# A Fourier layer and two expert layers on one core: expert blocks of 512 tokens, more steps of weight conversion for each unit, one subtraction on GpSimd

## The chip, the cores and the metric

One core of a Trainium2 chip runs the whole program. The metric is device time in microseconds (us) of one execution; a kernel's time is the median of several. All times here are in us unless marked ns. The engines are PE (matmuls), DVE (VectorE), ACT (ScalarE), POOL (GpSimd) and SP, which here issues every DMA.

## The reference, cut to what matters

```python
# x: (2, 3008, 256); expert weights 256 x 2048 and 2048 x 256, twice
X = rfft(x, axis=1)
Yr = Xr @ w_r - Xi @ w_i + b_r;  Yi = Xr @ w_i + Xi @ w_r + b_i
Y = soft_shrink(Yr, 0.01) + 1j * soft_shrink(Yi, 0.01)
x = irfft(Y).reshape(6016, 256)
h = x @ moe_w_in;   x = (h * cos(h)) @ moe_w_out
h = x @ moe2_w_in;  return (h * clip(h + 3, 0, 6) / 6) @ moe2_w_out
```

## The kernel before, in words

Nearly every matmul is done in three terms of split numbers: an operand is kept as a high part (rounded by ACT) and a low part (the rest, subtracted by DVE), and high*high, low*high and high*low are added up in PSUM.

**The Fourier half** runs once for each of two batches `b`. Sixteen `a_part`s (lines 329 to 344) make `zp` by the first DFT step and split it into `zh`, `zl`. Then come twelve steps `k2_step(b, p)` (lines 465 to 487). PE does 21 matmuls of 512 columns in each: two `w_mm` (tile `pp`, 6 each), one `v_mm` (tile `vp`, 3) and one `b_mm` (tile `bp`, 6). The other engines carry `bp` of step p-2 through the soft shrink: `bias_add` (DVE, line 426), `shrink_a` (ACT), `shrink_b` (DVE, 435), `shrink_hi` (ACT, makes `sh`, 440), `shrink_lo` (DVE, makes `sl`, 445). `v_mm(b, p)` reads `sh` and `sl` one step later, and `v_store` writes its result to DRAM. The twelve steps of a batch end in `drain`, whose pieces are dealt out among the next `a_part`s or, for the second batch, among the first expert units.

**The inverse DFT** is `y_part(g, ec)` (lines 281 to 302): 8 short matmuls into a buffer `yp` of the PSUM tag `h`, then split into token tiles `tok`. Sixteen groups g of 376 tokens, two halves each. `YP` says at which steps of the second batch the first of them stand; the rest stand among the expert units (`events`), shortly before the block that needs them.

**The expert half.** Tokens are cut into twelve blocks (`BLOCK_TOKENS`). A unit is 128 of the 2048 hidden features for one block in one expert layer m: `mm_h` (6 matmuls into `h`, line 578), four passes of ACT and DVE, and, four units later, `mm_out` (6 matmuls into `acc`, line 635). There are 16 units to a block and a layer, so 384 units. Order: blocks 0 and 1 of the first layer in turns of four units (`IL`), then block 2, then blocks (0, j) and (1, j-3) in turns of one unit, then the last three of the second layer.

**The weights** come as 64-bit numbers and are converted on the chip, 16 pieces of 512 KB for a layer. A piece takes five steps of `cv.step`: DVE operations `clamp` (153), `shift` (156), `top` (159), `exponent` (162), `rest` (165), with `magnitude` and `hi` on ACT (150, 169), and `rest`'s addition and `lo` on POOL (166, 172). `lo` of a piece, after which it counts as finished, comes in the fourth step of the next piece. Steps are dealt out by tables: `RATE_A` in the `a_part`s (one for each pair, from the last pair of the first batch on), `RATE_W` in the k2 steps below `PW` (an entry before `shrink_b`, then one of two in turn), `RATE_M` in the expert units. Where a unit needs a piece that isn't finished, `cv.require` issues the missing steps on the spot.

Each engine executes its instructions in the order in which they were put into its own queue. The orders shown below are those queues.

Of the kernel before, what the change touches and what calls it, by code (L numbers as in the profile page):

```python
# [12 lines left out]
I32 = mybir.dt.int32  # L13
U32 = mybir.dt.uint32
AF = mybir.ActivationFunctionType
ALU = mybir.AluOpType
# [11 lines left out]
LAM = 0.01  # L28
TWO_PI = 2.0 * math.pi
YPAIRS = 4  # L30
BLOCK_TOKENS = [502, 502, 500] * 4
A_CHUNKS = [4] * 8
NFC = DFF // 128
LEAD = 3
DELAY = 4
WARM = 9
IL, IM = 4, 1

RATE_M = (1, 1, 1, 1, 0, 0, 1, 0)
RATE_A = (0, 1)  # L40
RATE_W = (1, 1, 2)
LATE, CC, CV0 = [1, 3, 4], 5, 7
XB = 3
EG, PW = 0, 10
YP = (0, 2, 4, 6, 8)
YE = 3


# [64 lines left out]
def fourier_moe_moe_kernel(ctx, tc, x, w_r, w_i, b_r, b_i, ta, tg, fg, win1, wout1, win2, wout2, out):  # L113
    nc = tc.nc
    pe, act, dve, sp = nc.tensor, nc.scalar, nc.vector, nc.sync

    def f32(ap):
        return ap.bitcast(F32)

    persist = ctx.enter_context(tc.tile_pool(name="persist", bufs=1))  # L120
# [13 lines left out]

    def convert(src, dst_hi, dst_lo, name):

        raw = persist.tile([128, 512, 2], I32, tag="raw", bufs=2, name=f"raw{name}")
        a = persist.tile([128, 512], F32, tag="cva", bufs=2, name=f"cva{name}")
        b = persist.tile([128, 512], F32, tag="cvb", bufs=1, name=f"cvb{name}")
        au, bu = a.bitcast(U32), b.bitcast(U32)  # L140
        w_lo, w_hi = raw.bitcast(U32)[:, :, 0], raw.bitcast(U32)[:, :, 1]

        def load():
            if len(src.shape) == 2:
                sp.dma_start(raw.rearrange("p f two -> p (f two)"), src)
            else:
                sp.dma_start(raw.rearrange("p (a f) two -> p a (f two)", a=2), src)

        def magnitude():
            act.activation(a, raw.bitcast(F32)[:, :, 1], AF.Abs)  # L150

        def clamp():
            dve.tensor_scalar(a, a, T_MIN, T_MAX, op0=ALU.max, op1=ALU.min)

        def shift():
            dve.tensor_scalar(au, au, 3, 0x3FFFFFF8, op0=ALU.logical_shift_left, op1=ALU.bitwise_and)

        def top():
            dve.scalar_tensor_tensor(au, w_hi, 0xC0000000, au, op0=ALU.bitwise_and, op1=ALU.bitwise_or)

        def exponent():
            dve.tensor_scalar(bu, au, 0xFF800000, None, op0=ALU.bitwise_and)

        def rest():
            dve.scalar_tensor_tensor(b, w_lo, float(2.0**-52), b, op0=ALU.mult, op1=ALU.mult)
            nc.gpsimd.tensor_tensor(a, a, b, op=ALU.add)

        def hi():
            act.activation(dst_hi, a, AF.Copy)  # L169

        def lo():
            nc.gpsimd.tensor_tensor(dst_lo, a, f32(dst_hi), op=ALU.subtract)  # L172

        return dict(load=load, magnitude=magnitude, clamp=clamp, shift=shift, top=top, exponent=exponent, rest=rest, hi=hi, lo=lo)
# [72 lines left out]
    cv = Converter()  # L247
# [18 lines left out]
    def token_set(pool, i):  # L266
        return [[pool.tile([128, MAXT], F32R, name=f"tok{i}_{e}{z}") for z in range(2)] for e in range(2)]

    free_sets = [token_set(persist, i) for i in range(3)]

    def load_u(g):
        if g >= NG:
# [32 lines left out]
    with ExitStack() as actx:  # L305
        apool = actx.enter_context(tc.tile_pool(name="apool", bufs=1))
        with tc.manual_schedule(engines={mybir.EngineType.PE, mybir.EngineType.SP, mybir.EngineType.Activation}):
# [134 lines left out]

            def shrink_lo(b, p):
                sh, sl = sh_t[b, p]
                dve.tensor_tensor(sl, u_t.pop((b, p)), f32(sh), op=ALU.subtract)

            def v_mm(b, p):
                vp = psum.tile([128, 2, D], F32, tag="acc1", bufs=2, name=f"vp{b}_{p}")
# [82 lines left out]
                        load_x(NA + p - 6)  # L531
                pend = drain(b)
            pend.pop(0)()
            y_part(2, 0)
            pend.pop(0)()
            y_part(2, 1)
            pend.pop(0)()
            pend.pop(0)()


    mpool = ctx.enter_context(tc.tile_pool(name="mpool", bufs=1))
    with tc.manual_schedule(engines={mybir.EngineType.PE, mybir.EngineType.SP, mybir.EngineType.Activation}):
        free_sets += [token_set(mpool, i) for i in range(3, LEAD + 3)]


        groups = [[(0, 0), (0, 1)]] + [[(0, j)] for j in range(2, LEAD)]
        groups += [[(0, j), (1, j - LEAD)] for j in range(LEAD, NBLK)] + [[(1, j)] for j in range(NBLK - LEAD, NBLK)]
        order, units, events = [], [], {}
        for i, group in enumerate(groups):
            step = IL if i == 0 else IM  # L550
            g0, n0 = len(units), len(order)
            order += group
            for q in range(NFC // step):
                units += [(n0 + n, *job, q * step + f) for n, job in enumerate(group) for f in range(step)]
            size = len(units) - g0
            if i + 1 < len(groups) and groups[i + 1][0][0] == 0:
                parts = [(g, e) for g in groups_of(groups[i + 1][0][1]) for e in range(2)]
                for k, (g, e) in enumerate(reversed(parts)):
                    events.setdefault(g0 + size - YE - 2 * k, []).append(lambda g=g, e=e: y_part(g, e))
# [100 lines left out]
        G = len(units)  # L660
        for g in range(G + DELAY):
# [9 lines left out]
                split_g(g - 2)  # L671
            if 0 <= g - 1 < G:
                act2(g - 1)
            if g > EG:
                cv.step(RATE_M[g % 4])
            for f in pend[:2]:
                f()
            pend = pend[2:]
            if g < G:
                act_abs(g)  # L680
                if g > EG:
                    cv.step(RATE_M[4 + g % 4])
            if 0 <= g - DELAY < G:
                n2, m2, _, fc2 = units[g - DELAY]
                cv.require(("out", m2, fc2 // 2))
# [49 lines left out]
```

## Time and profile before

| | before |
|---|---|
| median of 3 runs | 1264.58 us (1263.5 to 1269.22) |
| profiled execution, its own time | 1263.34 us |
| its span in the trace | 1261.6 us |
| PE busy | 1241.5 us, 98% |
| DVE / ACT / POOL busy | 827.2 / 791.6 / 85.4 us |
| mean granted TensorE clock | 0.985 of full speed |

The span is that of the instructions; 1.7 us of the execution's own time lie outside of it. Busy is the time in which at least one instruction of the engine ran. In the views of the trace a row has the start and the length in us, the engine, the line of the kernel, the operation, and output<-inputs with partitions x elements; `xN` counts instructions, and `[t <-E tile]` is idle time before it with what ended that time.

### The profile page before, as it was taken

To read this page: it belongs to the slowest core of one execution; us is meant where nothing else is said; L and a number is where in the kernel's file an instruction comes from. 1 tells how busy PE (TensorE), PEld (TensorE's weight loads), DVE (VectorE), ACT (ScalarE), POOL (GpSimd) and SP (SyncE) were. 2 spreads that over 40 slices of the span, in tenths; PEclk is the share of its full clock that TensorE was granted. 3 is DMA by queue.
4 is the path that set the end of the run, shared out by engine and by line. 5 is a ranking of instruction groups with operands and counts; after the bars stand their busy time and mean duration, and the time that the engine had idled before them with its cause. 6 is when DMAs were issued, how large, how long until landed. Compare 5 with 4: busy or idle time off the path is not lost.

```text
span 1261.6 us, 15535 instructions
## 1 busy us (share of the span) xinstructions
PE 1241.5 (98%) x5633; PEld 1035.5 (82%) x5633; DVE 827.2 (66%) x1349; ACT 791.6 (63%) x1468; POOL 85.4 (7%) x68
## 2 busy tenths in 40 slices
PE   8999999999998999999999999999999999999998
PEld 7888878888876888888888888888888888888887
DVE  5988889998877655656556556556556556554444
ACT  5665679898775655656666566566666666653443
POOL 0212212222223000000000000000000000000000
PEclk7997999999998999999999999999999999999999
DMA  7354441112111000001001001001000000000000
GB/s 204 91 151 131 124 110 52 51 51 85 51 51 34 17 1 19 17 1 35 17 1 34 1 1 34 1 18 34 1 18 17 1 1 17 1 17 1 17 17 17
DMA packets 25117, 48.53 MB, mean 38 GB/s; under 512 B 2768, under 2 KB 15696, under 8 KB 25040
## 3 DMA queue, kind: packets, MB, share of 16 engines
q1 hardware_dynamic: 25040, 47.54, 13.0%
q8 instruction: 44, 0.72, 0.2%
q14 instruction: 33, 0.27, 0.1%
HBM read 35.08 MB, written 12.45 MB: 38 GB/s over the span
## 4 chain that ended last, share of the span: by engine, by line
PE 94%; DVE 2%; ACT 1%; DMA 1%; issue 1%; POOL 0%; SPq 0%; DVEq 0%; POOLq 0%; ACTq 0%
PE h L578 41%; PE acc L635 41%; PE pp L397 5%; PE bp L420 2%; PE zp L333 2%; PE yp L285 2%; PE vp L451 1%; DMA x<-in_x_dram 1%; DVE zl L344 1%; DVE gl L622 0%; POOL w2i L172 0%; ACT r L589 0%; DVE u L435 0%; ACT r L602 0%; SPq L324 0%
## 5 line engine op out<-in xcount | busy, mean ns | idle before, releaser
L613 DVE SCALAR_TENSOR_TENSOR h<-r,h 128x502 f32<-128x502 f32 (+1 forms) x192 | 131.4, 684 | 261.4 <-ACT r L594 261.3
L578 PE MATMUL h<-tok,w2i 128*128 128x502 f32 (+1 forms) x1152 | 293.7, 389 | 6.3 <-ACT w2i L169 4.8
L578 PE MATMUL h<-tok,w1i 128*128 128x502 f32 (+1 forms) x1152 | 294.4, 391 | 3.5 <-DVE gl L622 3.3
L635 PE MATMUL acc<-gh,w1o 128*128 128x502 f32 (+1 forms) x768 | 267.8, 389 | 0.0
L635 PE MATMUL acc<-gh,w2o 128*128 128x502 f32 (+1 forms) x768 | 267.8, 390 | 0.0
L578 PEld LDWEIGHTS h<-tok,w2i 128*128 128x128 f32 x1152 | 217.2, 189 | 52.3 <-ACT w2i L169 5.5
L622 DVE TENSOR_TENSOR gl<-h,gh 128x502 fp32r<-128x502 f32 (+1 forms) x384 | 258.7, 674 | 0.7 <-ACT gh L621 0.7
L578 PEld LDWEIGHTS h<-tok,w1i 128*128 128x128 f32 x1152 | 214.9, 188 | 46.4 <-DVE gl L622 4.6
L594 ACT ACTIVATE r<-h 128x502 f32<-128x502 f32 (+1 forms) x192 | 113.3, 590 | 183.1 <-PE h L578 182.5
L621 ACT ACTIVATE gh<-h 128x502 fp32r<-128x502 f32 (+1 forms) x384 | 225.2, 586 | 1.2 <-PE acc L635 1.0
L589 ACT ACTIVATE r<-h 128x502 int32<-128x502 f32 (+1 forms) x192 | 113.6, 592 | 149.3 <-PE h L578 146.9
L590 DVE SCALAR_TENSOR_TENSOR r<-r,h 128x502 f32<-128x502 int32 (+1 forms) x192 | 129.9, 677 | 117.0 <-ACT r L589 116.3
L635 PEld LDWEIGHTS acc<-gh,w2o 128*128 128x128 f32 x768 | 145.0, 189 | 28.9
L635 PEld LDWEIGHTS acc<-gh,w1o 128*128 128x128 f32 x768 | 144.5, 188 | 29.3
L635 PE MATMUL acc<-gl,w2o 128*128 128x502 f32 (+1 forms) x384 | 149.9, 390 | 0.0
L635 PE MATMUL acc<-gl,w1o 128*128 128x502 f32 (+1 forms) x384 | 149.7, 390 | 0.0
L602 ACT ACTIVATE r<-r 128x502 f32<-128x502 f32 (+1 forms) x192 | 120.1, 625 | 41.1 <-DVE r L590 41.1
L611 DVE TENSOR_TENSOR h<-r,h 128x502 f32<-128x502 f32 (+1 forms) x192 | 129.6, 675 | 0.0
L610 ACT ACTIVATE r<-r 128x502 f32<-128x502 f32 (+1 forms) x192 | 120.3, 627 | 0.0
L635 PEld LDWEIGHTS acc<-gl,w2o 128*128 128x128 f32 x384 | 72.5, 189 | 15.4
L635 PEld LDWEIGHTS acc<-gl,w1o 128*128 128x128 f32 x384 | 72.1, 188 | 15.6
L333 PE MATMUL zp<-ta,x 96*128 96x96 f32 x256 | 41.6, 338 | 5.5 <-DVE zl L344 4.1
(79 smaller groups left out, 912.3 us busy)
## 6 DMA issues: line engine op xcount, KB each, us to landing
x<-in_x_dram SPq DMA_DIRECT2D x16, 384.0 KB, 4.7
u_dram<-v SPq DMA_DIRECT2D x48, 128.0 KB, 2.4
u_sb<-u_dram SPq DMA_DIRECT2D x16, 384.0 KB, 3.8
raw0i<-in_win_dram SPq DMA_DIRECT2D x8, 512.0 KB, 4.3
raw0o<-in_wout_dram SPq DMA_DIRECT2D x8, 512.0 KB, 3.9
raw1i<-in_win_dram SPq DMA_DIRECT2D x8, 512.0 KB, 3.6
raw1o<-in_wout_dram SPq DMA_DIRECT2D x8, 512.0 KB, 3.7
out_dram<-o SPq DMA_DIRECT2D x16, 251.0 KB, 2.1
```

The lines of the kernel that those rows point to most:

```text
L333: pe.matmul(zp[:, i * ROWS : (i + 1) * ROWS], lhsT=x_t[a][:, i, kc * 128 : (kc + 1) * 128], rhs=ta_t[a][:, i * ROWS : (i + 1) * ROWS], sta ...
L578: pe.matmul(hp[:, :t], lhsT=w[:, c0 : c0 + 128], rhs=r[:, :t], start=(i == 0), stop=(i == 5))
L589: act.activation(k[:, :t], hp[:, :t], AF.Copy, bias=0.0, scale=1.0 / TWO_PI)
L590: dve.scalar_tensor_tensor(r[:, :t], k[:, :t], -TWO_PI, hp[:, :t], op0=ALU.mult, op1=ALU.add)
L594: act.activation(r[:, :t], hp[:, :t], AF.Relu, bias=3.0, scale=1.0)
L602: act.activation(mid[g][:, :t], mid[g][:, :t], AF.Abs)
L610: act.activation(r[:, :t], r[:, :t], AF.Sin, bias=math.pi / 2, scale=-1.0)
L611: dve.tensor_tensor(hp[:, :t], r[:, :t], hp[:, :t], op=ALU.mult)
L613: dve.scalar_tensor_tensor(hp[:, :t], r[:, :t], 6.0, hp[:, :t], op0=ALU.min, op1=ALU.mult)
L621: act.activation(gh[:, :t], hp[:, :t], AF.Copy)
L622: dve.tensor_tensor(gl[:, :t], hp[:, :t], f32(gh[:, :t]), op=ALU.subtract)
L635: pe.matmul(acc[n][d][:, :t], lhsT=w[:, fc % 2, d * 128 : (d + 1) * 128], rhs=r[:, :t], start=(fc == 0 and i == 0), stop=(fc == NFC - 1 an ...
```

## The change

- `BLOCK_TOKENS` becomes eleven blocks of 512 tokens and one of 384 (6016 in all, as before). A token tile has 512 columns instead of 502.
- The first group is no longer two blocks in turns: blocks 0, 1, 2 of the first layer run one after the other.
- Only the first two groups of `y_part` (four parts) stand before the expert units, at steps 3 and 6 and after the drain's first two pieces; before, it was three groups (six parts).
- `RATE_W` is (1, 2, 2) for all twelve steps (`PW` 12): three conversion steps for each k2 step instead of 2 or 3 in ten of twelve. In the expert units the rate is 7 steps for 8 units while blocks 0 to 2 run, then one for a unit of the first layer and two for one of the second.
- The raw weights have three buffers instead of two.
- `shrink_lo` runs on POOL instead of DVE.

```diff
-BLOCK_TOKENS = [502, 502, 500] * 4
+BLOCK_TOKENS = [512] * 11 + [384]
...
-IL, IM = 4, 1
-RATE_M = (1, 1, 1, 1, 0, 0, 1, 0)
 RATE_A = (0, 1)
-RATE_W = (1, 1, 2)
+RATE_W = (1, 2, 2)
+RATE_1 = ((1, 0),) * 7 + ((0, 0),)
+RATE_2 = ((1, 0), (1, 1))
...
-EG, PW = 0, 10
-YP = (0, 2, 4, 6, 8)
+PW = 12
+YP = (0, 3, 6)
...
-        raw = persist.tile([128, 512, 2], I32, tag="raw", bufs=2, name=f"raw{name}")
+        raw = persist.tile([128, 512, 2], I32, tag="raw", bufs=3, name=f"raw{name}")
...
-    free_sets = [token_set(persist, i) for i in range(3)]
+    free_sets = [token_set(persist, i) for i in range(2)]
...
-                dve.tensor_tensor(sl, u_t.pop((b, p)), f32(sh), op=ALU.subtract)
+                nc.gpsimd.tensor_tensor(sl, u_t.pop((b, p)), f32(sh), op=ALU.subtract)
...
-            y_part(2, 0)
+            y_part(1, 0)
             pend.pop(0)()
-            y_part(2, 1)
+            y_part(1, 1)
...
-        groups = [[(0, 0), (0, 1)]] + [[(0, j)] for j in range(2, LEAD)]
+        groups = [[(0, j)] for j in range(LEAD)]
...
-            step = IL if i == 0 else IM
...
-            for q in range(NFC // step):
-                units += [(n0 + n, *job, q * step + f) for n, job in enumerate(group) for f in range(step)]
+            for q in range(NFC):
+                units += [(n0 + n, *job, q) for n, job in enumerate(group)]
...
-            if g > EG:
-                cv.step(RATE_M[g % 4])
+            rate = (0, 0)
+            if g < G:
+                rate = RATE_1[g % 8] if units[g][2] < LEAD and units[g][1] == 0 else RATE_2[units[g][1]]
+            cv.step(rate[0])
...
-                if g > EG:
-                    cv.step(RATE_M[4 + g % 4])
+                cv.step(rate[1])
```

In the changed file the lines of the Fourier half stand one further down (`bias_add` is line 427, `shrink_lo` 446), those of the expert half one further up.

The first place is DVE's queue in the k2 steps of the first batch. The names: `bp` bias_add, `u` shrink_b, `ph` the low part of a `pp`, `sl` shrink_lo, `cva`/`cvb` conversion. Before:

```order
L426 TENSOR_TENSOR bp_3_487<-bp_3_487,bias 128x512
L162 TENSOR_SCALAR cvb0o_369<-cva0o_368 128x512
L165 SCALAR_TENSOR_TENSOR cvb0o_369<-raw0o_367,cvb0o_369 128x512
L435 SCALAR_TENSOR_TENSOR u_3_504<-bp_3_487,u_3_504 128x512
L411 TENSOR_TENSOR ph_0_5_495<-pp_10_496,ph_0_5_494 128x512
L445 TENSOR_TENSOR sl_3_515<-u_3_504,sh_3_514 128x512
L426 TENSOR_TENSOR bp_4_535<-bp_4_535,bias 128x512
L411 TENSOR_TENSOR ph_0_5_495<-pp_11_522,ph_0_5_494 128x512
L435 SCALAR_TENSOR_TENSOR u_4_552<-bp_4_535,u_4_552 128x512
```

And in the changed kernel, around `bp` 5 and 6:

```order
L427 TENSOR_TENSOR bp_5_594<-bp_5_594,bias 128x512
L412 TENSOR_TENSOR ph_0_6_548<-pp_13_576,ph_0_6_547 128x512
L157 TENSOR_SCALAR cva0i_511<-cva0i_511 128x512
L436 SCALAR_TENSOR_TENSOR u_5_615<-bp_5_594,u_5_615 128x512
L412 TENSOR_TENSOR ph_0_7_606<-pp_14_607,ph_0_7_605 128x512
L160 SCALAR_TENSOR_TENSOR cva0i_511<-raw0i_510,cva0i_511 128x512
L163 TENSOR_SCALAR cvb0i_512<-cva0i_511 128x512
L166 SCALAR_TENSOR_TENSOR cvb0i_512<-raw0i_510,cvb0i_512 128x512
L412 TENSOR_TENSOR ph_0_7_606<-pp_15_633,ph_0_7_605 128x512
L427 TENSOR_TENSOR bp_6_645<-bp_6_645,bias 128x512
L436 SCALAR_TENSOR_TENSOR u_6_666<-bp_6_645,u_6_666 128x512
```

The `sl` rows have left DVE's queue, and more conversion rows stand between the shrink's.

The second place is POOL's queue in the same steps, which holds only conversion before (the additions of `rest`, and `lo`):

```order
L166 TENSOR_TENSOR cva0i_249<-cva0i_249,cvb0i_250 128x512
L166 TENSOR_TENSOR cva0o_368<-cva0o_368,cvb0o_369 128x512
L172 TENSOR_TENSOR w1i_68<-cva0i_249,w1i_67 128x512
L166 TENSOR_TENSOR cva0o_459<-cva0o_459,cvb0o_460 128x512
L172 TENSOR_TENSOR w1o_82<-cva0o_368,w1o_81 128x512
```

And in the changed kernel:

```order
L167 TENSOR_TENSOR cva0o_343<-cva0o_343,cvb0o_344 128x512
L446 TENSOR_TENSOR sl_3_522<-u_3_505,sh_3_521 128x512
L167 TENSOR_TENSOR cva0o_434<-cva0o_434,cvb0o_435 128x512
L173 TENSOR_TENSOR w1o_82<-cva0o_343,w1o_81 128x512
L446 TENSOR_TENSOR sl_4_569<-u_4_557,sh_4_568 128x512
L446 TENSOR_TENSOR sl_5_626<-u_5_615,sh_5_625 128x512
L173 TENSOR_TENSOR w1o_84<-cva0o_434,w1o_83 128x512
```

Each `sl` now stands among the conversion's operations, here `sl_4` behind two of them.

The third place is ACT's queue where the expert units begin; `r` and `gh` are tiles of the first units, `sh_11` and `u_11` of the last shrink. Before:

```order
L431 ACTIVATE u_11_1661<-bp_11_1628 128x512
L589 ACTIVATE r_1721<-h_1714 128x502
L440 ACTIVATE sh_11_1725<-u_11_1661 128x512
L602 ACTIVATE r_1721<-r_1721 128x502
L589 ACTIVATE r_1736<-h_1729 128x502
```

And in the changed kernel:

```order
L432 ACTIVATE u_11_1685<-bp_11_1652 128x512
L588 ACTIVATE r_1757<-h_1750 128x512
L170 ACTIVATE w1o_93<-cva0o_1431 128x512
L441 ACTIVATE sh_11_1763<-u_11_1685 128x512
L601 ACTIVATE r_1757<-r_1757 128x512
L588 ACTIVATE r_1774<-h_1767 128x512
```

One `hi` of the conversion has come to stand among the first unit's operations.

## Rows read from the trace of the kernel before

**Rows 1.** The page: busy time of each engine with its share of the span, and the granted TensorE clock in tenths, in 40 slices of the span.
```profile
PE 1241.5 (98%) x5633; PEld 1035.5 (82%) x5633; DVE 827.2 (66%) x1349; ACT 791.6 (63%) x1468; POOL 85.4 (7%) x68
PEclk7997999999998999999999999999999999999999
```

**Rows 2.** Busy time by stretch of the span: the stretch, its length, then busy time (and instructions) of PE, PEld, DVE, ACT and POOL, the granted clock, the DMA share and GB/s.
```profile
40.00:80.00 40.00, 40.00 (x176) 32.83 (x175) 36.50 (x62) 26.51 (x49) 10.61 (x8) 1.00 0.46 128
...
360.00:400.00 40.00, 33.65 (x139) 26.53 (x138) 30.93 (x51) 23.56 (x44) 13.52 (x10) 0.91 0.14 40
...
440.00:480.00 40.00, 40.00 (x177) 33.04 (x177) 23.16 (x38) 24.41 (x45) 0.00 (x0) 1.00 0.00 1
```

**Rows 3.** The chain of work that ended last, in order of time, in the k2 steps of the first batch: one step.
```profile
43.61 1.39 PE pp L397 x6
45.00 1.36 PE bp L420 x6
46.36 1.36 PE pp L397 x6
47.72 0.70 PE vp L451 x3
```

**Rows 4.** The same chain in the expert half: a unit of 502 tokens, and one of 500.
```profile
453.43 1.38 PE acc L635 x6
454.81 1.35 PE h L578 x6
...
1224.27 1.34 PE acc L635 x6
1225.61 1.35 PE h L578 x6
```

**Rows 5.** The timeline at 377 us, PE's rows.
```profile
377.21 0.38 PE L635 MATMUL acc<-gh,w1o 128*128 128x502 f32 x1
378.98 0.72 PE L578 MATMUL h<-tok,w2i 128*128 128x502 f32 x2 [1.38 <-ACT w2i L169]
380.87 0.50 PE L578 MATMUL h<-tok,w2i 128*128 128x502 f32 x1 [1.16 <-POOL w2i L172]
384.74 1.21 PE L578 MATMUL h<-tok,w2i 128*128 128x502 f32 x2 [3.37 <-ACT w2i L169]
386.29 0.79 PE L578 MATMUL h<-tok,w2i 128*128 128x502 f32 x1 [0.34 <-POOL w2i L172]
...
389.39 1.81 PE L578 MATMUL h<-tok,w1i 128*128 128x502 f32 x6
391.04 0.39 PE L635 MATMUL acc<-gh,w1o 128*128 128x502 f32 x1
```

**Rows 6.** The timeline of the k2 steps of the first batch, rows of DVE and, last, the matmul that reads `sl`.
```profile
57.98 0.42 DVE L153 TENSOR_SCALAR cva0o<-cva0o 128x512 f32<-128x512 f32 x1
58.43 0.69 DVE L411 TENSOR_TENSOR ph<-pp,ph 128x512 fp32r<-128x512 f32 x1
...
62.35 0.69 DVE L165 SCALAR_TENSOR_TENSOR cvb0o<-raw0o,cvb0o 128x512 f32<-128x512 uint32 x1
62.96 0.68 DVE L435 SCALAR_TENSOR_TENSOR u<-bp,u 128x512 f32<-128x512 f32 x1
...
64.34 0.69 DVE L445 TENSOR_TENSOR sl<-u,sh 128x512 fp32r<-128x512 f32 x1
65.62 0.70 DVE L426 TENSOR_TENSOR bp<-bp,bias 128x512 f32<-128x512 f32 x1 [0.59 <-PE bp L420]
...
67.02 0.39 PE L451 MATMUL vp<-sl,fgr 128*128 128x512 f32 x1
```

**Rows 7.** The timeline at three places at which DVE and POOL run at once.
```profile
63.18 1.30 POOL L166 TENSOR_TENSOR cva0o<-cva0o,cvb0o 128x512 f32<-128x512 f32 x1 [6.11 <-DVE cvb0o L165]
63.56 0.68 DVE L411 TENSOR_TENSOR ph<-pp,ph 128x512 fp32r<-128x512 f32 x1
...
192.76 1.29 POOL L172 TENSOR_TENSOR w1o<-cva0o,w1o 128x512 fp32r<-128x512 f32 x1 [8.33 <-ACT w1o L169]
192.92 1.41 DVE L162 TENSOR_SCALAR cvb0i<-cva0i 128x512 uint32<-128x512 uint32 x1
...
384.76 1.47 POOL L172 TENSOR_TENSOR w2i<-cva1i,w2i 128x512 fp32r<-128x512 f32 x1 [0.74 <-ACT w2i L169]
385.14 1.64 DVE L165 SCALAR_TENSOR_TENSOR cvb1o<-raw1o,cvb1o 128x512 f32<-128x512 uint32 x1
```

**Rows 8.** The timeline where the expert units begin: the fifth unit's first matmuls, and an operation of the conversion on ACT.
```profile
182.39 1.62 PE L578 MATMUL h<-tok,w1i 128*128 128x502 f32 x6 [1.58 <-DVE gl L622]
182.40 0.65 ACT L169 ACTIVATE w1o<-cva0o 128x512 fp32r<-128x512 f32 x1
```

**Rows 9.** The timeline of PE around two parts of the inverse DFT, one behind the other, in the first expert units.
```profile
247.88 1.03 PE L285 MATMUL yp<-tg_sb,u_sb 96*128 96x94 f32 x8
249.73 1.62 PE L578 MATMUL h<-tok,w1i 128*128 128x502 f32 x6 [0.82 <-DVE gl L622]
...
255.26 1.03 PE L285 MATMUL yp<-tg_sb,u_sb 96*128 96x94 f32 x8
256.07 1.61 PE L578 MATMUL h<-tok,w1i 128*128 128x502 f32 x6
```

More of the change, by code (lines that the diff above doesn't have):

```diff
@@ L542, in fourier_moe_moe_kernel @@
     with tc.manual_schedule(engines={mybir.EngineType.PE, mybir.EngineType.SP, mybir.EngineType.Activation}):
-        free_sets += [token_set(mpool, i) for i in range(3, LEAD + 3)]
-        groups = [[(0, 0), (0, 1)]] + [[(0, j)] for j in range(2, LEAD)]
+        free_sets += [token_set(mpool, i) for i in range(2, LEAD + 3)]
+        groups = [[(0, j)] for j in range(LEAD)]
         groups += [[(0, j), (1, j - LEAD)] for j in range(LEAD, NBLK)] + [[(1, j)] for j in range(NBLK - LEAD, NBLK)]
```

## The prediction

> **What bounds the kernel now.** The page's first part comes first: PE is busy 98% of the span and no other engine over 66% [rows 1]. So the end moves only if PE runs fewer or shorter matmuls, or if it loses less time to waiting and to the lower clock. The change leaves the number of matmuls as it is. The stretches show where PE is not full: from 440 to 480 us it runs 177 matmuls at full clock, from 360 to 400 only 139, at a granted clock of 0.91 [rows 2]. The k2 steps are full as well, but there DVE is busy 36.50 of 40 us [rows 2]: an engine that is not the bound and has little to spare. The chain of work gives the rhythm: a k2 step takes 1.39 + 1.36 + 1.36 + 0.70 = 4.81 us [rows 3], an expert unit of 502 tokens 2.73, one of 500 2.69 to 2.71 [rows 4].
>
> **The gap at 377 us, and what the faster conversion does to it.** From 377.21 to 391.04 PE gets through 19 matmuls of 502 columns [rows 5]. At 2.73 / 12 = 0.2275 each they need 4.3, so 13.8 - 4.3 = 9.5 us are lost: idle 6.2, the rest matmuls that start 0.4 apart after the idle, where the stretch's clock has fallen. The rows name who ended the waits: `hi` (ACT) and `lo` (POOL) of a weight piece `w2i`. Counting steps tells why. Before the first unit stand 1 + 8 + 2 x 25 = 59 steps, then 1.25 for each unit. Unit 73 is the first that reads the last quarter of `w2i`, pieces 29 and 30 of 32; piece 30 is finished with step 30 x 5 + 4 = 154, and 59 + 1.25 x 72 is 149. Five steps short: `require` issues them on the spot and PE waits through the whole piece. In the changed kernel 1 + 8 + 2 x 36 = 81 steps stand before the first unit, 42 come in units 0 to 47, then 1.5 for each unit: 154 is reached at unit 69, three units (8 us) early. The first layer's weights have their 80 steps before the units begin, so that running block 0 alone, which takes them twice as fast, costs nothing. Gain: **-9.5**.
>
> **Longer blocks.** Matmuls and columns are as many as before, but time does not go by columns: six of 512 columns take 1.36 us (`bp`) or 1.36 to 1.39 (`pp`) [rows 3], where six of 502 take 1.35 (`h`) and 1.38 (`acc`) [rows 4]. Three of `vp` take 0.70, or 1.40 for six [rows 3]. `vp` reads `sh` and `sl`, which lie in the very buffers (tags `gh`, `gl`) that `mm_out` reads. So I take 1.365 for `h` and 1.40 for `acc`, 2.765 for a unit of 512. The block of 384 has no row; with three quarters of 2.765 (2.07) as the lower bound and 128 columns less at 1/2.4 ns each (2.765 - 0.64 = 2.125) as the upper, I take 2.10. Before: 32 units x (8 x 2.73 + 4 x 2.70) = 1044.5. After: 32 x (11 x 2.765 + 2.10) = 1040.5. That is **-4**; if `acc` went like `bp` it would be 32 x 11 x 0.04 = 14 less, and if `h` went like the slower `pp` (1.39) 9 more.
>
> **Subtraction on GpSimd and three steps for each k2 step.** Rows of DVE that take 0.69 start 0.61 apart, rows of 0.42 start 0.45 apart [rows 6]. A piece is 3 x 0.45 + 2 x 0.61 = 2.57, a step 0.51. Before, DVE has 5 x 0.61 + 2.5 x 0.51 = 4.3 for a k2 step; after, 4 x 0.61 + 3 x 0.51 = 3.97, so that 0.84 of 4.81 are free. On DVE's own account the move pays for the conversion. But POOL takes 1.30 for a subtraction or addition [rows 7], so it gets 1.30 + 3/5 x 2 x 1.30 = 2.86 for a step, 59%, where it had 1.30. And the two engines get in each other's way: an `exponent` of DVE that begins 0.16 after a POOL operation takes 1.41, where operations of its kind take 0.42, and ends 0.28 after it; a `rest` takes 1.64 instead of 0.69 [rows 6, 7]. A `ph` beside POOL takes 0.68, as ever [rows 7]: what reads PSUM isn't held up. So each of the three conversion operations of a step finds POOL at work with a chance of 0.59 and then waits half of 1.30: 3 x 0.59 x 0.65 = 1.15. That is 0.31 over the 0.84 that are free. Twenty k2 steps carry both (the first two of a batch have no shrink yet): **+6**. The lower end is 0 (the waits fall into idle time), the upper comes from waits as long as the one shown (about 1.0, so 1.77 for a step): 0.93 x 20 = 19. A second way to the same loss is the path of `sl`: now it ends at 65.03 and `vp` reads it at 67.02 [rows 6], 2.0 spare. On POOL it takes 0.6 longer, and one operation in front of it 1.3 more; with two in front, as `sl_4` has them, 1.2 are missing. Queued behind that `vp` is all of PE.
>
> The Trainium skill (SBUF — State Buffer, section Who interferes with whom) says that DVE instructions in a two-port mode or with two SBUF inputs and GpSimd's share a port pair as an exclusive lock, and that whoever issues first keeps it for the whole instruction. That is what the rows show. Taken only as a budget, the rule asks for 3 x 0.51 + 2.86 = 4.4 of port time in a step of 4.81 and would charge nothing, which is the first rival's time; it does not say how two queues in fixed order share it.
>
> **Smaller things.** Where units begin, the fifth unit waits 1.58 for the first unit's `gl` [rows 8], at the end of a chain through ACT; a `hi` of 0.65 [rows 8] now stands in that chain: **+0.6** (0 to 2, since `y_part(1, 1)` is also needed by the very first unit now). The first `y_part` of a cluster among single units costs 1.85, the second 0.81 [rows 9]. There are three such clusters instead of two: **+1** (0 to 2). The third raw buffer and six more small splits lie beside PE's work: nothing, as long as ACT and DVE keep their gaps in the units.
>
> **Sum.** -9.5 - 4 + 6 + 0.6 + 1 = -5.9. Against the profiled execution's own 1263.3 that is 1257.4; the median of the three runs shown is 1.2 above it, so I say 1258.5.
>
> **The rivals.**
> - *The port costs nothing* (the k2 step stays at 4.81): the terms without +6 give 1251 to 1253. For it: DVE has 0.84 to spare and the port's sum is below a step. Against it: both queues are in fixed order, and the port would be taken 91% of the time.
> - *`acc` takes 1.36 too*: 14 less, 1244. For it: six matmuls of 512 columns do go in 1.36 [rows 3]. Against it: the only rows that read those buffers, `vp`, don't.
> - *Slower: the k2 steps become DVE's and POOL's.* If nearly every conversion operation waits a full POOL operation and `sl` comes late on top, the step goes to about 5.9: 20 x 1.1 = 22, which gives 1275. It decides from 5.75 for a step on, where the loss passes 19. For it: at 384.76 both engines do just this, operation by operation [rows 7]. Against it: 2.44 of DVE's work in a step don't touch the port and can run beside POOL.
> - *The wait for `w2i` stays* (a piece is late for another reason, such as its load): 1268. The count leaves three units, so this is unlikely.
>
> **How the numbers follow.** About 0.5% (6.3 us) is what a measurement of this kernel can tell from no change, so faster means below 1258.3 and slower above 1270.9. The forecast's mechanism, with k2 losing 3 to 16 us (1255 to 1268), gets 0.51, spread from its lower end; the first rival (1250 to 1255) 0.24; the second (1242 to 1250) 0.10; the slower one 0.13; the last 0.02. Faster: 0.24 + 0.10 and 0.14 of the forecast's own, 0.48. Slower 0.13, the same 0.39. The range 1246 to 1271 leaves out the slower rival and half of the second: 0.18. The forecast's own range is 1255 to 1268.
>
> **What would show it.** Right: no PE wait on `w2i`, and no gap at unit 73; six `acc` of 512 in 1.40 and six `h` in 1.36 to 1.37; k2 steps on the chain of 4.9 to 5.5, with conversion rows of DVE over 1.0 us beside POOL's and waits of `vp` on POOL `sl`. Wrong: k2 steps of 4.81 to the end (the +6 falls), six `acc` in 1.36 (the -4 is too small), or PE below full clock in the k2 steps after such waits, which the sum does not hold at all.

## The result: 1.1% slower

The changed kernel takes **1279.64 us** (median of four runs, 1276.8 to 1281.3); the kernel before took 1265.45 beside it. The ratio is **1.0106, 95% interval 1.0074 to 1.0138**, 14 us more where 6 less were forecast. It lies above the range of 1246 to 1271.

The page of the changed kernel, its parts 1, 2 and 4 (busy time, the granted clock in tenths, the chain that ended last):
```profile
PE 1258.8 (98%) x5633; PEld 1039.5 (81%) x5633; DVE 823.9 (64%) x1331; ACT 789.0 (62%) x1474; POOL 116.3 (9%) x92
PEclk9996999999999999999999999999999999999999
PE 90%; DVE 6%; ACT 2%; issue 1%; DMA 1%; POOL 0%; SPq 0%; POOLq 0%; ACTq 0%; DVEq 0%
```
Against [rows 1] PE still shows 98% with as many instructions, and DVE is less busy than before; what moved is POOL, from 85.4 to 116.3. The shares do not show the loss, the chain does: 6% of it is DVE's, where it was 2% before:
```profile
PE 94%; DVE 2%; ACT 1%; DMA 1%; issue 1%; POOL 0%; SPq 0%; DVEq 0%; POOLq 0%; ACTq 0%
```
The three stretches of [rows 2] again:
```profile
40.00:80.00 40.00, 37.69 (x162) 29.75 (x160) 33.38 (x51) 23.78 (x45) 21.27 (x16) 1.00 0.39 100
360.00:400.00 40.00, 40.00 (x174) 32.40 (x173) 34.26 (x61) 27.73 (x51) 10.22 (x8) 1.00 0.15 50
440.00:480.00 40.00, 40.00 (x174) 32.37 (x173) 23.24 (x37) 24.11 (x45) 0.00 (x0) 1.00 0.04 14
```
The gap is gone: from 360 to 400 us PE runs 174 matmuls where it ran 139. But in the k2 steps it runs 162 where it ran 176, at full clock, and DVE gets through 51 operations instead of 62 (a k2 step has 4 + 3 of them now where it had 5 + 2.5, so 58 at the old pace). The chain in those steps, with its pieces on DVE:
```profile
60.99 1.36 PE pp L398 x6
62.35 0.72 PE vp L452 x3
...
66.24 1.30 POOL w1o L173
67.56 0.67 ACT cva0i L151
68.26 0.78 DVE cva0i L154
...
72.40 1.42 DVE cvb0i L163
73.84 1.67 DVE cvb0i L166
75.51 0.60 DVE ph L412
76.11 0.62 DVE bp L427
76.75 0.61 ACT u L432
77.38 0.70 DVE u L436
```
Up to 63 us the chain is PE's, step by step as in [rows 3]; from there to 94 us, the end of batch 0's steps, it has not one more piece on PE. Two conversion operations that took 0.42 and 0.69 [rows 6] take 1.42 and 1.67, and `ph`, `bp` and `u` stand behind them. Just before, DVE is idle for 2.1 us: its `clamp` at 68.26 waits for ACT's `magnitude`, and that for POOL's `lo` at 66.24. (e1, below, has such a wait of 1.9 too, and PE loses 0.1 by it.) Steps that took 4.81 take 6.5, 5.3, 6.0 and 5.3 from the eighth on. At 67 us `vp` reads `sh` and then waits for `sl`; the timeline of POOL and PE there:
```profile
64.98 1.30 POOL L167 TENSOR_TENSOR cva0o<-cva0o,cvb0o 128x512 f32<-128x512 f32 x1 [3.41 <-DVE cvb0o L166]
66.24 1.29 POOL L173 TENSOR_TENSOR w1o<-cva0o,w1o 128x512 fp32r<-128x512 f32 x1
67.00 0.40 PE L452 MATMUL vp<-sh,fgr 128*128 128x512 f32 x1
67.49 1.26 POOL L446 TENSOR_TENSOR sl<-u,sh 128x512 fp32r<-128x512 f32 x1
...
68.81 0.50 PE L452 MATMUL vp<-sl,fgr 128*128 128x512 f32 x1 [1.41 <-POOL sl L446]
```
The addition of `rest` and the `lo` of a weight piece stand in front of `sl`: 2.6 us, and PE waits 1.41 of them.

Where the 17.4 us between the two profiled executions lie, by the starts of PE's rows in the two timelines (each stage from its first matmul to the first of the next; us). The kernels of the experiments stand below, by their labels:
```
                start  k2 of b0  a of b1  k2 of b1,  units   units   unit 80   span    median
                                          drain      0-47    48-79   to end            time
before          29.2   55.5      25.9     63.2      135.9   98.6    853.4    1261.6   1265.5
after           33.3   61.7      34.3     68.8      139.2   91.0    850.8    1279.0   1279.6
e1_lo_dve       28.6   55.7      29.1     61.1      140.2   91.0    850.8    1256.5   1262.5
e2_rate_w       31.5   58.8      28.3     63.5      141.2   91.0    850.6    1264.9   1265.3
e3_before_lo    30.5   58.4      27.7     64.7      135.9   99.1    853.0    1269.2   1271.2
e6_vp_later     28.4   58.3      31.9     65.5      139.4   91.0    850.5    1265.0   1270.5
e8_dummy_pool   32.0   65.2      33.2     75.9      140.2   91.0    850.5    1288.1   1290.4
e9_store_act    28.5   62.5      25.4     75.9      144.4   91.0    850.5    1278.2   1279.9
e13_store_b0    32.6   63.3      25.4     69.7      139.2   91.0    850.5    1271.7   1273.6
e14_cv_paused   31.0   61.0      32.8     68.9      142.3   91.0    850.5    1277.6   1280.4
e4_aligned      31.9   61.4      33.8     68.9      138.3   89.5    841.3    1265.1   1266.1
e5 (e1 + e4)    31.3   56.6      28.0     60.9      139.4   89.5    841.3    1247.0   1249.8
```
"start" is the a-stage of batch 0, "a of b1" that of batch 1. Two `y_part` left the k2 stage of batch 1 for the units, which takes about 2 us from the one and gives them to the other. A row is one execution: those of e1 and e6 are about 4 us below the medians of their kernels.

### The profile page after: what moved, and what is told of

It reads as the page before. It is cut to its first block, busy times and chain, and to the rows that moved or that the text cites. A ratio compares the mean times of both kernels' runs of the same rounds, so it can differ in the third digit from the quotient of the medians.

```text
span 1279.0 us, 15606 instructions
## 1 busy us (share of the span) xinstructions
PE 1258.8 (98%) x5633; PEld 1039.5 (81%) x5633; DVE 823.9 (64%) x1331; ACT 789.0 (62%) x1474; POOL 116.3 (9%) x92
## 4 chain that ended last, share of the span: by engine, by line
PE 90%; DVE 6%; ACT 2%; issue 1%; DMA 1%; POOL 0%; SPq 0%; POOLq 0%; ACTq 0%; DVEq 0%
PE acc L634 41%; PE h L577 40%; PE zp L334 3%; PE pp L398 2%; PE yp L286 2%; DMA x<-in_x_dram 1%; DVE ph L412 1%; PE bp L421 1%; DVE bp L427 1%; DVE u L436 1%; DVE cvb0i L166 1%; PE vp L452 1%; DVE cvb0o L166 0%; ACT u L432 0%; DVE cva0o L154 0%
## 5 line engine op out<-in xcount | busy, mean ns | idle before, releaser
L612 DVE SCALAR_TENSOR_TENSOR h<-r,h 128x512 f32<-128x512 f32 (+1 forms) x192 | 131.4, 685 | 261.8 <-ACT r L593 261.7
L577 PE MATMUL h<-tok,w1i 128*128 128x512 f32 (+1 forms) x1152 | 294.2, 391 | 1.8 <-DVE gl L621 1.7
L577 PE MATMUL h<-tok,w2i 128*128 128x512 f32 (+1 forms) x1152 | 291.6, 388 | 0.0
L634 PE MATMUL acc<-gh,w1o 128*128 128x512 f32 (+1 forms) x768 | 270.2, 392 | 0.0
L634 PE MATMUL acc<-gh,w2o 128*128 128x512 f32 (+1 forms) x768 | 269.5, 392 | 0.0
L621 DVE TENSOR_TENSOR gl<-h,gh 128x512 fp32r<-128x512 f32 (+1 forms) x384 | 258.3, 673 | 0.8 <-ACT gh L620 0.8
L620 ACT ACTIVATE gh<-h 128x512 fp32r<-128x512 f32 (+1 forms) x384 | 224.7, 585 | 0.8 <-PE acc L634 0.5
L634 PE MATMUL acc<-gl,w2o 128*128 128x512 f32 (+1 forms) x384 | 149.2, 389 | 0.0
L634 PE MATMUL acc<-gl,w1o 128*128 128x512 f32 (+1 forms) x384 | 149.2, 388 | 0.0
L601 ACT ACTIVATE r<-r 128x512 f32<-128x512 f32 (+1 forms) x192 | 120.0, 625 | 37.6 <-DVE r L589 37.5
L609 ACT ACTIVATE r<-r 128x512 f32<-128x512 f32 (+1 forms) x192 | 120.2, 626 | 0.0
```

What stands on the lines that cost most here:

```text
L577: pe.matmul(hp[:, :t], lhsT=w[:, c0 : c0 + 128], rhs=r[:, :t], start=(i == 0), stop=(i == 5))
L601: act.activation(mid[g][:, :t], mid[g][:, :t], AF.Abs)
L609: act.activation(r[:, :t], r[:, :t], AF.Sin, bias=math.pi / 2, scale=-1.0)
L612: dve.scalar_tensor_tensor(hp[:, :t], r[:, :t], 6.0, hp[:, :t], op0=ALU.min, op1=ALU.mult)
L620: act.activation(gh[:, :t], hp[:, :t], AF.Copy)
L621: dve.tensor_tensor(gl[:, :t], hp[:, :t], f32(gh[:, :t]), op=ALU.subtract)
```

## The experiments

**Each of the two edits undone (e1, e2), and the one alone (e3).** e1 is the changed kernel with
```
-                nc.gpsimd.tensor_tensor(sl, u_t.pop((b, p)), f32(sh), op=ALU.subtract)
+                dve.tensor_tensor(sl, u_t.pop((b, p)), f32(sh), op=ALU.subtract)
```


> The changed kernel with one line undone: shrink's subtraction for `sl` is on DVE again; the faster conversion in the k2 steps stays. Theory A (the subtraction on POOL is what costs: its `sl` comes late and it takes the port from DVE's conversion): the k2 stage of batch 0 falls from 61.7 us to 55 to 57, that of batch 1 by 6 as well, the a-stage of batch 1 (34.3 us, of which the late `v` stores and the late x loads are a part) to 26 to 29; in all 1256 to 1264 us. Theory B (the three conversion steps cost: their loads, POOL's additions and DVE's own time): DVE has 5 x 0.61 + 3 x 0.51 = 4.6 of 4.81 us to do in a step, so the k2 stages stay above 60 and 67 us and the time above 1272. Theory C (neither; PE is slower there because its clock is): the stages stay as in the changed kernel, 1275 to 1281.

Measured: 1262.46 us, ratio to before 0.9968 (0.9950 to 0.9986), faster than before. k2 of batch 0 takes 55.7. The stretch from 40 to 80 us in e1:
```profile
40.00:80.00 40.00, 40.00 (x176) 32.39 (x175) 36.47 (x64) 27.54 (x52) 13.67 (x10) 1.00 0.56 150
```
PE is full again with 176 matmuls and DVE does 64 operations in 36.47 us, against 51 in 33.38. Three conversion steps for each k2 step cost these steps nothing; the subtraction on POOL costs the changed kernel 17 us.

e2 leaves it on POOL and takes the conversion back:
```
-RATE_W = (1, 2, 2)
+RATE_W = (1, 1, 2)
-PW = 12
+PW = 10
-                rate = RATE_1[g % 8] if ...
+                rate = (1, int(g < NFC)) if ...
```


> The changed kernel with the conversion in the k2 steps as slow as before (2.5 steps for each, in the first ten); the subtraction stays on POOL. So that no weight is late, block 0 alone converts two steps in each of its units instead of 7/8, which brings the count back to 123 at unit 48. Theory A (the subtraction on POOL costs): POOL still has 1.30 + 1/2 x 2 x 1.30 = 2.6 of 4.81 us in a step, so most of the loss stays: k2 of batch 0 at 59 to 62 us, the time 1273 to 1281. Theory B (the added steps cost): k2 of batch 0 at 55 to 57 us, a-stage of batch 1 at 26 to 29, the time 1256 to 1264. If each does a part, about 1268.

Measured: 1265.33 us, 0.9995 (0.9979 to 1.0011). That too gives back 14 of the 17, where theory A wanted nearly nothing. So neither edit costs that by itself; the two together do. e3, the kernel before with the subtraction on POOL alone:

> The kernel before with one part of the change alone: shrink's subtraction for `sl` on POOL. Theory A: the k2 stages lose most of what they lose in the changed kernel (batch 0 from 55.5 to 59 to 62 us), the a-stage of batch 1 too, and the time is 1273 to 1284 us. Theory B: below 1268 us, k2 of batch 0 at 55 to 57, since DVE is freed of 0.6 us a step and nothing is added. Theory C (the clock alone): 1262 to 1267 too, unless its profile shows PE at half speed where the matmuls are spaced 0.21 instead of 0.11.

Measured: 1271.23 us, 1.0046 (1.0030 to 1.0061): 5 us, below theory A's 1273 to 1284, above theory B's. In e2 the DVE rows of `shift` and of `exponent` for the pieces in `cva0i`, from 30 to 90 us (min, median and max in ns):
```profile
L157 DVE TENSOR_SCALAR cva0i<-cva0i x3: 428/1535/1536, 34.0 to 74.8; 128x512 uint32<-128x512 uint32 x3
L163 DVE TENSOR_SCALAR cvb0i<-cva0i x3: 410/416/417, 35.8 to 77.6; 128x512 uint32<-128x512 uint32 x3
```
With 2.5 steps one operation of a piece meets POOL in the steps of batch 0 and takes 1.5 us instead of 0.42, the next have their own time. With three it happens there to two in a row, as at 72.40 above, and DVE does not catch up.

**A late `sl`, or the port (e6, e8).** e6 gives `sl` one step more:
```
-                if p >= 3:
-                    v_mm(b, p - 3)
+                if p >= 4:
+                    v_mm(b, p - 4)
```
(the store likewise, and the drain takes the pair that is left over.)

> The changed kernel (subtraction on POOL) with the three `vp` matmuls of a pair and its store one k2 step later, so that `sl` has 4.81 us more before PE asks for it. DVE, POOL and the port do the same work as in the changed kernel. Theory A1 (the loss is PE waiting for a late `sl`): no wait of `vp` for POOL, k2 of batch 0 from 61.7 to 55 to 58 us, the time 1262 to 1270. Theory A2 (the loss is DVE being held at the shared port, so that its `ph`, `u` and `bp` come late): the waits move to `bp` on DVE `ph`, k2 of batch 0 stays at 59 to 62, the time 1273 to 1281.

Measured: 1270.5 us, 1.0027 (1.0008 to 1.0046), 9 less than the changed kernel, k2 of batch 0 58.3. PE's waits on batch 0's steps, first the changed kernel's (30 to 93 us), then e6's (30 to 85):
```profile
PE vp L452 <- POOL sl L446: 3.1, 3, 1.4
PE bp L421 <- DVE ph L412: 0.4, 2, 0.2
```
```profile
PE bp L421 <- DVE ph L412: 1.6, 2, 0.9
```
The wait for `sl` is gone, and a smaller one for `ph` has come. Both theories have a share: giving `sl` more time returns about half of the 17 (3.4 and 3.3 in the two k2 stages, 2.4 in the a-stage between them). That what is left is the port's, and the pair's that moved into the drain, is argued.

e8 has POOL do the subtraction for nobody:
```
-                nc.gpsimd.tensor_tensor(sl, u_t.pop((b, p)), f32(sh), op=ALU.subtract)
+                u = u_t.pop((b, p))
+                dve.tensor_tensor(sl, u, f32(sh), op=ALU.subtract)
+                if free_sets:
+                    nc.gpsimd.tensor_tensor(free_sets[-1][1][1], u, f32(sh), op=ALU.subtract)
```


> The changed kernel with `sl` on DVE again, but POOL does the same subtraction as well, at the place where it did it, into a tile that nobody reads: the same 1.30 us of POOL and the same port, with no matmul behind it, and DVE has its 0.61 us back too (4.6 of 4.81 us in a step, as in the first experiment). Theory A1 (late `sl`): as the first experiment, k2 of batch 0 at 54 to 56 us, 1260 to 1266. Theory A2 (port): k2 of batch 0 at 59 to 64 us and batch 1 alike, 1272 to 1284, with conversion rows of DVE of 1.3 us and more.

Measured: 1290.36 us, 1.0186 (1.0151 to 1.0222), 28 more than e1, more than theory A2 had. POOL's work at the port is expensive without a matmul behind it, the more so as DVE's own `sl`, which `vp` needs, has to share the port as well. With that `sl` DVE has 0.61 more to do in each step than in the changed kernel, so the 28 is not the port's share of the 17. e8's timeline, and the row of its `sl`:
```profile
61.01 0.68 DVE L447 TENSOR_TENSOR sl<-u,sh 128x512 fp32r<-128x512 f32 x1
61.03 1.81 POOL L449 TENSOR_TENSOR tok<-u,sh 128x512 fp32r<-128x512 f32 x1 [1.59 <-ACT sh L441]
61.60 1.52 DVE L157 TENSOR_SCALAR cva0o<-cva0o 128x512 uint32<-128x512 uint32 x1
```
```profile
L447 DVE TENSOR_TENSOR sl<-u,sh x24: 681/869/1811, 45.2 to 211.6; 128x512 fp32r<-128x512 f32 x24
```
DVE began 0.02 earlier and kept its 0.68, while POOL took 1.81; the next operation of DVE then waited for POOL in turn. The Trainium skill (SBUF — State Buffer, section Who interferes with whom) says just that of issue order, and these rows agree, as [rows 7] did.

**The a-stage of batch 1 (e9, e13, e14).** It went from 25.9 to 34.3 us. SP's queue and PE in the changed kernel:
```profile
90.76 7.11 SPq L459 DMA_DIRECT2D u_dram<-v  x4
...
99.42 0.40 SPq L327 DMA_DIRECT2D x<-in_x_dram  x1
```
```profile
114.24 1.99 PE L334 MATMUL zp<-ta,x 96*128 96x96 f32 x8 [2.78 <-DMA x<-in_x_dram]
```
The first of these rows is four stores of `v`, each of which stands in SP's queue until its `v` is made; x loads stand behind them, and PE waits 2.78 for one. SP's waits for `v` from 76 to 125 us, in the kernel before and in the changed one (total, times, longest):
```profile
SPq L458 <- ACT v L456: 9.7, 3, 3.5
```
```profile
SPq L459 <- ACT v L457: 20.4, 4, 7.6
```
They have doubled. But PE's wait is hardly new: e1, where no `sl` is late, has one of 2.40 for x, and the kernel before one of 2.51 at the same place, which its trace puts to `zl` while the x load lands at the same time. e9 issues all these stores from ACT, e13 those of batch 0 alone; e13's edit, where e9 has `act` in every case:
```
-                    sp.dma_start(
+                    (act if b == 0 else sp).dma_start(
```


> The changed kernel with the stores of `v` (L459) issued by ACT, right behind the `v` that they wait for, instead of by SP, where x loads, raw loads and loads of `u` queue behind them. Theory D (a part of the a-stage of batch 1, 34.3 us against 25.9, is x loads that stand behind a store that waits for a late `v`): the wait of `zp` for x (2.8 us at 114.2) goes, the a-stage of batch 1 falls to 29 to 32 us, the time to 1274 to 1278. Rival: the x loads are late for their buffers, or PE only waits at the next place (`bp` for `ph`) and at the lower clock all the same: the a-stage stays at 33.5 to 35, the time 1277 to 1282; above that, if ACT's issuing takes it from the k2 steps.

Measured: 1279.94 us. The stage fell to 25.4, further than expected, and the rival's time came: the k2 steps and the drain of batch 1 took 7 more and the first units 5.

> The changed kernel with the stores of `v` of batch 0 alone issued by ACT. Theory D (x loads behind the store of a late `v` make the a-stage of batch 1 long, by waits and by the lower clock after them): that stage takes 25 to 29 us instead of 34.3, the later ones stay: 1271 to 1276. Rival E (conversion work of ACT and POOL in front of `ph` and `sh` makes it long): 32 to 35 us, the time 1277 to 1282.

Measured: 1273.59 us, 1.0050 (1.0032 to 1.0069), 6 less than the changed kernel, stage 25.4. The stage in the changed kernel and in e13, and the row of `zp` in each:
```profile
95.00:129.30 34.30, 28.62 (x145) 26.21 (x143) 24.07 (x32) 19.30 (x29) 10.06 (x8) 0.66 0.57 149
L334 PE MATMUL zp<-ta,x x128: 247/421/498, 95.0 to 129.2; 96*128 96x96 f32 x128
```
```profile
96.00:121.30 25.30, 19.59 (x144) 17.33 (x142) 20.98 (x29) 18.09 (x29) 7.86 (x7) 1.00 0.61 171
L334 PE MATMUL zp<-ta,x x128: 246/275/351, 95.9 to 119.7; 96*128 96x96 f32 x128
```
The same work keeps PE busy 28.62 us at a granted clock of 0.66 and 19.59 at 1.00: these 9 us are the difference of the stage. PE's idle time is the same in both, 5.7 us, in shorter pieces in e13. In the changed kernel PE waited for `ph` and for x and was then at 1.2 GHz in part of the stage, at 421 ns for a `zp` instead of 275; in e13 it stayed at 2.4 GHz. The kernel before was between the two:
```profile
84.60:110.50 25.90, 23.21 (x144) 22.06 (x144) 22.62 (x32) 17.68 (x25) 2.64 (x3) 0.80 0.72 193
```
Its PE is idle for 2.7 us and busy for 23.2, so that the 8.4 us are 3.0 of idle time and 5.4 of the lower clock.

e14 takes the conversion out of the stage:
```
-                        if b > 0 or c >= CV0:
+                        if b == 0 and c >= CV0:
-                rate = RATE_1[g % 8] if ...
+                rate = (1, int(g < 9)) if ...
```


> The changed kernel with no conversion in the a-stage of batch 1 (its 8 steps come in the first 9 units). Theory D: the stage stays at 32 to 35 us, since the stores still stand in front of the x loads; 1278 to 1282. Rival E: `ph` comes without its wait for ACT at 98.7 us, the stage takes 28 to 31 us, 1274 to 1278; two to three us less of it if the first units pay, as in the other kernel with this edit (12.4 us from the first `h` to the first `acc` instead of 11.1).

Measured: 1280.38 us, stage 32.8. The conversion in this stage is not what makes it long. Theory D's stages and times came in both, e13 and e14, but its reason is shown only in part: with the stores moved the stage is at full clock (e9 too), not with less idle time; e15 below has the stores moved as well, and its clock is low all the same.

**Blocks and placement (e4, e7, e11).** e7 is e1 with the old blocks:
```
-BLOCK_TOKENS = [512] * 11 + [384]
+BLOCK_TOKENS = [502, 502, 500] * 4
```


> The kernel of the first experiment (the changed kernel with `sl` on DVE, 1262.5 us) with the old blocks of 502, 502 and 500 tokens: what the block sizes alone are worth. The prediction's term (six `h` of 512 in 1.365 us, six `acc` in 1.40) has 512 worth 4 us, so that this kernel would take 1265 to 1268. The paces in the traces since (`h` 230.6 and `acc` 233.6 ns at 512 columns, 174.1 and 173.4 at 384; 226.5 and 228.4 at 502, 225.9 and 224.3 at 500) make 32 x (11 x 2.785 + 2.085) = 1047.0 against 1044.4: then this kernel is 2.6 faster, 1258 to 1261.

Measured: 1262.21 us, 0.9975 (0.9962 to 0.9988), e1's own time. The longer blocks gain nothing. The chain in the units of the changed kernel, to be held against 1.35 and 1.38 of 502 columns in [rows 4]:
```profile
445.11 1.39 PE h L577 x6
446.50 1.40 PE acc L634 x6
```
e4 moves `gh`, `gl`, `sh` and `sl` by 32 bytes:
```
-            first = persist.tile([128, 2], F32, name="first")
+            first = persist.tile([128, 16], F32, name="first")
...
-        tt = persist.tile([ROWS, YT], F32, tag="tg_sb", name=f"tg_sb{g}")
+        tt = persist.tile([ROWS, YT + 8], F32, tag="tg_sb", name=f"tg_sb{g}")
```


> The changed kernel with its SBUF tiles moved by 32 bytes: `first` is 64 bytes wide instead of 8 and `tg_sb` 1536 instead of 1504, so that `gh`, `gl` (`sh`, `sl`), which began 32 bytes past a multiple of 64, begin on one; no instruction is added or removed. Theory: the second rival of the prediction had the cause of `acc`'s slower pace open; a row of 512 elements that begins off a multiple of 64 bytes touches 33 pieces of 64 bytes instead of 32, and 234 ns of `acc` against 227 of `bp` are just that ratio. Then `acc` (512) goes from 234 to 227 to 228 ns: 2112 matmuls x 6.5 = 13.7 us less, and `vp` (236) 72 x 8 = 0.6 less: 1264 to 1268 us. Rival: the pace of `acc` comes from what else is read and written meanwhile (or from `acc` being in other PSUM banks than `h`): no change, 1277 to 1282.

Measured: 1266.12 us, 1.0004 (0.9993 to 1.0015), 13.5 less than the changed kernel, where the theory had 14.3. The row of `acc` on `gh`, from 420 us to the end, in the changed kernel and in e4:
```profile
L634 PE MATMUL acc<-gh,w2o x720: 334/397/401, 420.3 to 1275.2; 128*128 128x512 f32 x164, 128*128 128x384 f32 x16
```
```profile
L634 PE MATMUL acc<-gh,w2o x716: 333/389/398, 422.4 to 1261.3; 128*128 128x512 f32 x163, 128*128 128x384 f32 x16
```
A median of 397 ns becomes 389, and from start to start the 512-column `acc` go from 233.6 to 228.8 on the mean. The whole is not `acc`'s alone: `h`, whose tiles lay well already, went from 230.6 to 229.3.

e11 is e7 with e4's tiles:

> The kernel with the old blocks, and its SBUF tiles moved by 32 bytes as before, so that `gh` and `gl` begin on a multiple of 64; `tok` tiles lie as in the kernel beside it. Theory (pieces of 64 bytes): a row of 502 or 500 elements touches 32 pieces from either place, so nothing moves but `vp` (512): `acc` at 228 and 224 ns, the time within 2 us of the kernel beside it. Rival (a start off a multiple of 64 costs by itself): `acc` falls by 5 to 7 ns, 2304 matmuls x 6 = 14 us less.

Measured: 1260.6 us, 0.9962 (0.9948 to 0.9977), 1.6 below e7, within the 2 that the theory allows and far from the rival's 14. That a row's 64-byte pieces are what is counted fits all four kernels (512 and 502 columns, each from both places); it was not seen directly.

**Combinations (e5, e10, e12, e15).** e5 is e1 with e4's tiles.

> The changed kernel with both findings of the first runs: `sl` is subtracted on DVE (1262.5 us alone) and the tiles are moved by 32 bytes (13.5 us less alone). If the two are independent, as theory has it, since one acts in the k2 steps and the other in `acc` and `vp`: 1262.5 - 13.5 = 1249, so 1247 to 1252, with `acc` (512) at 228 to 229 ns and k2 of batch 0 at 54 us. If they are not (a quicker unit leaves ACT and DVE too little room for the conversion): 1253 to 1260, with new waits of PE in the units.

Measured: **1249.82 us, 0.9868 (0.9844 to 0.9892)**: the two gains add up, and this beats both kernels. Three tries to shorten its a-stage of batch 1 as well. e10 issues the drain's stores of batch 0 from ACT, e12 pauses the conversion in that stage besides, e15 issues all of batch 0's stores from ACT:

> The kernel with `sl` on DVE and the tiles moved (1249.8 us), with the last three stores of `v` of batch 0 alone issued by ACT. When all stores were, the a-stage of batch 1 took 25.4 us instead of 34.3, all its `zp` at 0.11, but k2 of batch 1 and what follows took 10 us more. Theory D (x loads that stand behind the store of a late `v`, and the lower clock after the waits that this makes): the a-stage of batch 1 goes from 28.0 to 25 to 26, and no other stage moves: 1246 to 1248. Rival (the stage's length is where the clock happens to fall, as in the a-stage of batch 0, 28.3 to 33.3 us in ten profiles of the same instructions): 27 to 30 again, 1248 to 1251.

> As the kernel beside it, and the conversion pauses in the a-stage of batch 1 (its 8 steps are made in the first 9 units instead). Theory: the wait of 1.7 us of `bp` for ACT's `ph` at 86.0 us, which the faster conversion brings (ACT stands behind a `cva` that waits for POOL), goes: a-stage of batch 1 about 24 to 25 us, 1244 to 1247. Rival: the first units, which convert one step more each, lose it again: 1246 to 1250.

> The kernel with `sl` on DVE and the tiles moved (1249.8 us), with the stores of `v` of batch 0 alone issued by ACT. Theory D: the a-stage of batch 1 from 28.0 to 25 to 26 us, the time 1246 to 1248. Rival E: 27 to 29 us and 1248 to 1251.

Measured: 1247.15 (0.9861, 0.9833 to 0.9889), 1249.11 (0.9868, 0.9844 to 0.9893) and 1248.96 us (0.9866, 0.9849 to 0.9883); the stage took 27.8, 27.0 and 28.1 us, against 28.0 in e5. The four are not told apart, and theory D fails here. Its first half came true: e5's PE waits 2.5 us before a `zp` (the trace puts it to `sl`, the x load lands at the same time), and in e15 no wait for x is left and none of the stage is longer than 1.1. Its second half did not; e15's stage and PE's longest waits in it:
```profile
87.30:115.40 28.10, 24.40 (x144) 22.47 (x144) 24.61 (x34) 17.69 (x28) 5.51 (x4) 0.78 0.57 162
PE zp L334 <- DVE zl L345: 2.1, 3, 1.1
```
The granted clock is 0.78, and 48 of the 128 `zp` take over 350 ns, where one does in e13; yet e13's waits are as long (1.0 for `ph`, 1.4 at the end of its stage). What decides the clock of this stage stays open.

## Why the prediction was wrong, point by point

- **The gap, -9.5: right, with a count that was four steps too high.** The first two steps of a batch skip the entry before `shrink_b`, so a batch converts 23 and 34 steps there, not 25 and 36, and 55 and 77 stand before the units, not 59 and 81. Before, unit 73 was nine steps short and not five, and both `w2i` pieces were late, which is why `hi` and `lo` stand twice in [rows 5]; in the changed kernel step 154 comes in unit 71, two units early and not three. The conclusion holds: units 48 to 79 went from 98.6 to 91.0 us; the longer blocks add 32 x 0.056 = 1.8 there, which leaves 9.4. PE no longer waits for a `w2i`: where unit 73 begins (406.9 us) the chain of [rows 5] now reads as anywhere else in the units:
```profile
405.63 1.40 PE acc L634 x6
...
408.42 1.40 PE acc L634 x6
409.82 1.39 PE h L577 x6
```
- **Blocks, -4: wrong, the term that failed is `h`.** `acc` was sized right (6 x 233.6 = 1.40), the block of 384 too (2.085 for 2.10). `h` was not: 1.384 instead of 1.365. So 32 x (11 x 2.785 + 2.085) = 1047.0, against 1044.4 for the old paces: +2.6 where -4 stood, and e7 measures about 0. `bp`'s pace [rows 3] was carried over to `h`, which reads other tiles. Why `h` is slower than `bp` stays open, and so does why e7's `h` of 502 takes 228.7 ns where the kernel before had 226.5.
- **The k2 steps, +6: the mechanism is there, its balance failed.** The steps lose 6.0 us in batch 0 and 4.1 in batch 1 (against e1, which has the same `y_part`), 10 in all; 0.8 and 0.6 of these are each batch's first step, still at the low clock of the stage before. The drain loses 3.6 more. The waits at the port are no larger than forecast: of the 63 conversion rows of DVE in the changed kernel's k2 steps 22 take over 0.1 us longer than their kind takes unheld, 16.6 us in all (e1: 5 of 64, 2.6 us), where 1.15 for each of twenty steps is 23. The step that failed is what was set against them, the 0.84 us that are free in every step: by that balance 16.6 costs nothing, since twenty steps have 16.8 free. But the waits do not come evenly. They come two in a row (1.42 and 1.67 in the chain above), DVE is idle for ACT at other moments, and the last five steps carry nearly all that batch 0 loses by waits. The second step that failed is the path of `sl` with "two in front": it was named, with 1.2 us missing, and had no term. PE waited 1.41 for it at 67 us, and in the whole kernel (total, times, longest):
```profile
PE vp L452 <- POOL sl L446: 5.6, 5, 2.2
```
  e6 gives this path about half of the loss. The slower rival had 5.9 for all twenty steps, nearly the time of the eighth to the eleventh, but by waits of nearly every operation, and a third of them waited.
- **A stage that the sum left out.** The a-stage of batch 1 took 8.4 us more: 3.2 with the faster conversion alone (e1), 5.2 with the subtraction on POOL. The sum looked at the k2 steps only and asked of the late `sl` who waits on PE, not who stands behind `v` in SP's queue. "PE below full clock after such waits" was named as what would make the prediction wrong, for the k2 steps; it came in the a-stage behind them. e13 brings the stage to 25.4 and the time 6 us down. It does so by the clock alone, and the kernel before, at 25.9, was not at full clock there either.
- **The smaller things, +1.6: nothing of it came.** PE's waits for `gl` in the whole kernel are no longer than the one of 1.58 in [rows 8] (total, times, longest):
```profile
PE h L577 <- DVE gl L621: 1.7, 2, 1.3
```
  Units 0 to 47 take 3.3 us more, less than the two `y_part` moved there (2.1) and the longer blocks (48 x 0.056 = 2.7) account for, so the third cluster [rows 9] has cost nothing that can be seen.
- **The start, +4.2 in the profile: not the change's.** The instructions there are the same, and in the seventeen profiles of this study the first `pp` begins anywhere from 28.4 to 33.3 us. The rest of the profiled executions' 17.4 is 13.2; the medians differ by 14.2.

What took the time out of the range: the k2 steps and their drain (14 us by the profiles where +6 stood), the a-stage (8 where nothing stood) and the blocks (about 0 where -4 stood). Summed up by runs: without the subtraction on POOL the change gains 3.5 us (e1) where the sum without its +6 had 11.9; with it comes 17.2 instead of 6.

## What to carry to other kernels

Before an operation is moved to an engine that is idle on average, look at what already stands in its queue at that moment and who reads the result: two operations in front of it held PE for 1.4 us at a time here, and the price jumps when a second stream on the same engine is quickened, so that two edits must be costed together. Follow a late result past its first reader, into the stores that wait for it and the loads queued behind them, and into the next stage, whose clock may be lower after it. Where the bound is matmuls, look at where their moving tiles begin before changing how long they are: here 32 bytes were worth 13.5 us, more than the gap that the change closed.

## What the runs showed of the hardware

- `acc` of 512 fp32r columns goes at 233.6 ns when the row of its moving tile begins 32 bytes past a multiple of 64, at 228.8 when it begins on one (e4); 502 columns hardly differ (228.2 in e7, 227.7 in e11).
- The a-stage of batch 0 is the same instructions in every kernel, and PE runs more or less of it slowly. The row of `zp` up to 33 us in the changed kernel and in e1:
```profile
L334 PE MATMUL zp<-ta,x x127: 420/421/499, 5.5 to 33.0; 96*128 96x96 f32 x127
```
```profile
L334 PE MATMUL zp<-ta,x x128: 275/275/499, 5.2 to 28.5; 96*128 96x96 f32 x128
```
  The Trainium skill (TensorE: Matmul & The Clock Gate, section What's actually happening) says that when the clock rises varies from run to run with where the first matmul falls in the time that the chip watches. These profiles agree that it varies; whether the first matmul's place is the reason, none of them shows. The record of the granted clock reads 1.00 in this stage of the changed kernel, though its `zp` take 421 ns all through, as those at a granted 0.66 do; the durations are to be trusted before it there.
